# Gated attention and MLP: where the last weights land, and when small steps of the schedule are issued

## The chip, the cores and the metric

The kernel runs on one core of a Trainium2 chip. A core has a matrix engine (TensorE, "PE" in the profile; its weight loads are listed apart as "PEld"), a vector engine (VectorE, "DVE"), a scalar engine for activations (ScalarE, "ACT"), GpSimd ("POOL"), and a queue processor (SyncE, "SP") that in this kernel issues nearly all DMA transfers. Sixteen DMA engines move the data. The engines run their own instruction streams in order and wait for each other by semaphores. The metric is the device time of one execution, in microseconds (us), as the median of several runs.

## What is computed

The input is one sequence of 2048 tokens of width 576. The output mixes softmax attention with 32 heads of 18 and a layer-normed MLP of hidden width 4608, token by token, by a sigmoid gate:

```
x = A_x
g = _sigmoid((x * gate_w).sum(-1, keepdims=True))
a = _A_ref(x, A_wqkv, A_wo)                       # softmax(q k^T / sqrt(18)) v, then @ wo
b = _B_ref(x, B_w1, B_b1, B_w2, B_b2)             # layernorm, gelu(y @ w1 + b1) @ w2 + b2
return g * a + (1 - g) * b
```

## The kernel before

Everything is float32 in and out. Where TensorE multiplies two activations or weights, each of them is split into a rounded part ("hi", type fp32r) and the remainder ("lo"), and three products hi x hi, lo x hi, hi x lo are summed.

**Attention.** The loop at the end of the kernel runs over 32 units u (16 pairs of heads, each in two halves of 1024 queries) and 16 steps kc of 128 keys: 512 steps. Scores are computed twice. Pass 1 (`s1_round`, L197) is only for the row maxima, which DVE reduces from PSUM (L199); `s1_finish` gathers them (L207 to L210), `rows` transposes them (L214), ACT copies the transpose to the tile `mr` (L216), and DMAs write it into rows 54 and 55, and 118 and 119, of the unit's query tile `qa` (the helper `dma_r`, L112). With these rows pass 2 (`s2`, L238) yields scores with the maximum already subtracted, ACT takes the exponential (L240) into one of three buffers ("p" and "ring"), and `pv` (L255) multiplies with the values. When a unit is done, `o_store` copies its result (`oe`, L267), extracts the denominators by DMA (`dn<-oe`, L269), stores the numerators (L275) and some slots later takes the reciprocal on DVE (`spread`, L278), stores it (L279, `dn_scr`), and again some slots later spreads it over the rows of a scratch tensor (`wide`, L287).

**MLP.** It is written as a generator, `mlp()`, whose pieces fill PE between the attention's matmuls. It goes over 4 blocks of 512 tokens and in each over 9 groups of 4 chunks of 128 hidden units. A group has two up pairs q (`h_pair`, L433, 64x512 matmuls against the tile `big` that holds the normalised tokens) and four down tiles (`out_pair`, L513, accumulated by DVE at L522 in `x`). GELU is done by ACT (L484, L486) and POOL (helper `pool_op`, L153), which leaves `hh` and `hl`. In the first block the weights come raw from the input, and `split` prepares them: ACT rounds (L357, tile `w`), POOL subtracts (L153), the result serves the current block and is also stored in a scratch tensor (L362, `w_scr`) from which the other three blocks load it (`reload`, issued through L112, 1152 KB for an up pair, 576 KB for a down chunk). Up weights live in buffers of the pool `wp1`, down weights in those of `wp2`. Raw up weights are loaded at L336 into one half of a tile `x`, raw down weights at L342 into the other.

**What sets the order.** Every engine's order is the order in which the Python program emits instructions; nothing is rearranged. Three devices decide it. `run_due()` is called some four times per step and counts slots; `defer(n, f)` runs f at the n-th slot from now. `bg` is a list of weight splits: `run_due` takes one when the modelled end of POOL's work is near enough (`pool_end - now < queue`) and the slot that was written down when the raw weights were loaded, plus a constant, is reached (`LAND`, 8 slots, for up weights; `LAND - 2` for down weights). `ready()` takes entries at once when PE is about to use their result. `fill()` advances the MLP by one piece; when the MLP is used up it appends the output projection, `out_proj` (L1020 matmuls, its weights loaded at L880 and split at L873 and L874, its result combined with the MLP's by DVE at L1024).

SP's queue holds all the loads and stores in program order. Eight semaphores are used in turn for their completion, so that an issue waits for the transfer eight before it.

Of the kernel before, what the change touches and what calls it, by code (L numbers as in the profile page):

```python
# [8 lines left out]
F32 = mybir.dt.float32  # L9
F32R = mybir.dt.float32r  # L10
AF = mybir.ActivationFunctionType
# [5 lines left out]
P = 128  # L17
S = 2048
D = 576
# [3 lines left out]
NT = S // P  # L23
# [14 lines left out]
LEAD = 4  # L38
FILL = 1100.0
SLOT = 950.0  # L40
LAND = 8
GAP = 1130.0
TOTAL = NB * NG * (G // 2 * 27 * 231 + 8 * 3 * G * 131)
PLAN = [[(), (0,), (1,), (2,), (3,), (4,), (5, 6), ()], [(), (), (0,), (1,), (2,), (3,), (4,), (5, 6)],
# [2 lines left out]
PSTEP = (489, 494, 497, 499)  # L47
# [10 lines left out]
def gated_mix_kernel(ctx: ExitStack, tc: tile.TileContext, x, wqkv, wo, w1, b1, w2, b2, gate_w, out):  # L58
    nc = tc.nc
# [12 lines left out]
    w2_scr = dram.tile([NFC, P, 2, D], F32, name="w2_scr")  # L72
# [25 lines left out]
    def psum(pool):  # L98
        return pool.tile([P, TB], F32, name="ps")
# [10 lines left out]
    def dma_r(queue, dst, src):  # L110

        queue.dma_start(dst.bitcast(F32), src)  # L112


    slot = [0]
    later = []

    def defer(n, fn):
        later.append((slot[0] + n, fn))


    bg = []
# [27 lines left out]
    def pool_op(n, fn, *args, **kw):  # L150

        pool_end[0] = max(pool_end[0], now[0]) + n * (1.36 if fn == nc.gpsimd.tensor_scalar else 2.7)
        fn(*args, **kw)  # L153


    NU = 2 * NPAIR
# [5 lines left out]
    def unit(u):  # L162
        return UNITS[u]
# [37 lines left out]
    def s1_finish(u):  # L201

        m4 = M4.pop(u)
        nm = asm.tile([P, 2, 8], F32, name="nm")
        nm2 = asm.tile([P, 2, 2, 8], F32, name="nm2")
        nmh = asm.tile([P, 2, 8], F32R, name="nmh")
        nc.vector.tensor_reduce(nm, m4, axis=AX.X, op=ALU.max, negate=True)  # L207
        nc.vector.tensor_copy(nmh, nm)
        nc.vector.tensor_copy(nm2[:, :, 0, :], nmh.bitcast(F32))
        nc.vector.tensor_tensor(nm2[:, :, 1, :], nm, nmh.bitcast(F32), op=ALU.subtract)  # L210

        def rows():
            ps = psum(ps_s1)
            nc.tensor.transpose(ps[:32, :P], nm2.rearrange("p a b c -> p (a b c)"), ident)  # L214
            mr = asm.tile([32, P], F32R, name="mr", bufs=1)
            nc.scalar.activation(mr, ps[:32, :P], AF.Copy)  # L216
            qa = QA[u % 3]
            for h in range(2):
                for b in range(2):
                    r = 64 * h + 54 + b  # L220
                    k = (h * 2 + b) * 8
                    dma_r(nc.sync, qa[r:r + 1, :].rearrange("o (t n) -> o t n", n=P), mr[k:k + 8, :].bitcast(F32))
        if looped[0]:
            ROWS.append(rows)
        else:
            defer(2, rows)
# [35 lines left out]
    def o_store(u, ps):  # L262

        pair, half = unit(u)
        oe = asm.tile([P, TB], F32, name="oe", bufs=1)
        dn = asm.tile([P, 16], F32, name="dn", bufs=1)
        nc.vector.tensor_copy(oe, ps)  # L267
        cols = slice(2 * pair * DH, 2 * (pair + 1) * DH)
        nc.sync.dma_start(dn, oe[DH::32, :])  # L269
        for h in range(2):  # L270
            for qb in range(2):
                c = 32 * (2 * h + qb)
                d = (2 * pair + h) * DH
                q = half * HALF + qb * TB
                nc.sync.dma_start(ot_scr[0, d:d + DH, q:q + TB], oe[c:c + DH, :])  # L275

        def spread():
            nc.vector.reciprocal(dn, dn)  # L278
            nc.sync.dma_start(dn_scr[u], dn)  # L279
            if u < NU - 1:  # L280
                defer(16 if u < NU - 2 else 4, wide)
            else:
                hooks[0]()

        def wide():
            dst = ot_scr[1, cols, half * HALF:(half + 1) * HALF]
            nc.sync.dma_start(dst.rearrange("(h d) n -> h d n", d=DH), dn_scr[u][:, None, :].to_broadcast([2, DH, HALF]))  # L287
            stored.append(u)
        if u < NU - 1:
            defer(12 if u < NU - 2 else 4, spread)  # L290
        else:
            spread()

# [4 lines left out]
    looped = [False]  # L298
# [9 lines left out]
    def mlp():  # L308
        W1, W2, HT = {}, {}, {}
        RAW = {}  # L310
        seq = [(tb, g) for tb in range(NB) for g in range(NG)]
        n = len(seq)
# [3 lines left out]
        def chunk(q):  # L316

            i, m = divmod(q, G // 2)
            return i, m, seq[i][1] * G + 2 * m
# [5 lines left out]
        LOADED = {}  # L325
        NQ0 = npair // NB

        def load_w1(q):

            if (1, q) in LOADED or q >= NQ0:  # L330
                return
            LOADED[1, q] = slot[0] + (LAND if looped[0] else 5)
            fc = chunk(q)[2]
            for h in range(2):
                src = w1[:, (fc + h) * P:(fc + h + 1) * P]
                nc.sync.dma_start(R1[64 * h:64 * h + 64], src.rearrange("(c p) n -> p c n", p=64))  # L336

        def load_w2(c):
            if (2, c) in LOADED or c >= NFC:
                return  # L340
            LOADED[2, c] = slot[0] + (LAND - 2 if looped[0] else 3)
            nc.sync.dma_start(R2[c % 2], w2[c * P:(c + 1) * P, :])  # L342

        def rounded(dst, src):
# [7 lines left out]
        def split(table, key, pool, shape, raw, src, scr, then):  # L352

            def first():
                LOAD[raw[0]](raw[1])
                t = pool.tile(shape, F32R, name="w" + str(len(shape)))
                nc.scalar.activation(t[:, 0], src, AF.Copy)  # L357
                bg.insert(0, (any_time, lambda: second(t), queue))

            def second(t):  # L360
                pool_op(src.free_size(), nc.gpsimd.tensor_tensor, t[:, 1], src, t[:, 0].bitcast(F32), op=ALU.subtract)
                defer(4 if looped[0] else 20, lambda: nc.sync.dma_start(scr, t.bitcast(F32)))  # L362
                defer(3 if looped[0] else 1 if raw != (1, 2) else 16, lambda: then(raw[1]))
                table[key] = (t[:, 0], t[:, 1])

            queue = raw[0] ** 2 * SLOT
            bg.append((lambda: LOADED.get(raw, slot[0] + 1), first, queue))

        def reload(table, key, pool, shape, scr):
            t = pool.tile(shape, F32R, name=f"w{len(shape)}")  # L370
            dma_r(nc.sync, t, scr)
            table[key] = (t[:, 0], t[:, 1])
# [8 lines left out]
        def prep(upto):  # L381

            while asked[0] <= min(upto, npair - 1):
                q = asked[0]
                asked[0] += 1
                shape = [P, 2, 9, P]
                if q >= NQ0:
                    reload(W1, q, wp1, shape, w1_scr[q % NQ0])
                    continue
                split(W1, q, wp1, shape, (1, q), R1, w1_scr[q], lambda q: load_w1(q + 1))  # L390

        def prep_w2(i):
            for m in range(G // 2):
# [172 lines left out]
        def pair(q, ahead, last=False, inner=False):  # L566
            prep(q + ahead)
            yield from h_pair(q, last, inner)
            i, m, _ = chunk(q)
            if m == 1 and seq[i][1] == NG - 1:  # L570
                hidden[0] = seq[i][0]

        for i in range(n + 1):
            q = 2 * i
            inside = i < n and seq[i][1] == NG - 1
            held = 1 if 0 < i < n and seq[i][1] == 0 else 2
            if i < n:
                yield from pair(q, held, last=i > 0)  # L580
                prep(q + 1 + held)
            if i > 0:
                yield from outs(i - 1, pair(q + 1, 2, inner=True) if inside else ())
            if 0 < i < n:
                prep_w2(i)
            if i < n and not inside:
                yield from pair(q + 1, held)

    stream = [mlp()]
    spent = [0.0]  # L590
# [4 lines left out]
    kept = [0]  # L595

    def atom():

        while stream:
            try:  # L600
                spent[0] += next(stream[0])
            except StopIteration:
                stream.pop(0)
                return 0
            if cut[0]:
                end, cut[0] = cut[0], 0
                return end
        return 0
# [15 lines left out]
    with ExitStack() as a:  # L624
# [172 lines left out]
        for tb in range(NB):  # L797
            work = [(qk_group, (tb, mt)) for mt in (range(9) if tb < 2 else (4, 0, 1, 2, 3, 5, 6, 7, 8))] + [(v_group, (tb, t, n)) for t in range(4) for n in range(2)]
            for g, (fn, args) in enumerate(work):
                if tb == 0:  # L800
                    if g in W_AT:
                        n = W_AT[g]
# [19 lines left out]
                if tb == NB - 1:  # L822
# [5 lines left out]
                    if g == 9:  # L828
                        qkstack.close()
                        wp1 = mstack.enter_context(tc.tile_pool(name="m_w1", bufs=3))  # L830
# [211 lines left out]
    proj = out_proj()  # L1042
    over = [None]

    def fill(step, share):

        if over[0] is None:
            piece[0] = share
            behind[0] = base + (TOTAL - base) * step / FIN
            t = spent[0]  # L1050
            atom()
            run_due(max(spent[0] - t, GAP))
            if not stream and kept[0] == NT and step > PSTEP[-1] + 1:
                stream.append(proj)
                over[0] = step
                spent[0] = 0.0
        else:
            filler(spent[0] + FILL)
            run_due()

    looped[0] = True
    for u in range(NU):
        for kc in range(NT):
            step = u * NT + kc
# [63 lines left out]
```

## Time and profile before

| | us |
|---|---|
| time, median of 3 runs | 2394.49 |
| the runs | 2390.41, 2395.73, 2394.49 |
| span of the profiled execution | 2390.7 |
| the profiled execution's own time | not listed apart from the three runs |
| PE busy in the span | 2319.4 |
| DVE, ACT, POOL busy | 1650.7, 1364.9, 966.2 |
| mean granted PE clock | 0.99 |

The span runs from the first to the last instruction that the profiler recorded. A row of the timeline has the start, the duration, the engine, the line, the operation, what it writes and reads, the number of instructions that it stands for, and in brackets the idle time of that engine before it and what ended it. A row of the windows has the stretch, its length, the busy time of PE, PEld, DVE, ACT and POOL with counts, then the mean granted clock of PE (1.00 is full), the busy share of the DMA engines and the rate of the transfers in GB/s. "SPq" rows are issues of transfers; their duration is the time that the issue held SP's queue.

### The profile page before, as it was taken

The page shows a single profiled execution, that of the slowest core. Times are in us where ns is not written, and L with a number is a line of the kernel's source. Part 1 is how long each engine was busy: PE and PEld are TensorE (multiplying, and loading weights), DVE is VectorE, ACT ScalarE, POOL GpSimd, SP SyncE. Part 2 cuts the span into 40 slices and gives each one's busy share as a digit, 9 for nine tenths or more (in the row PEclk, how much of TensorE's full clock was granted, in tenths as well). Part 3 has the DMA queues.
Part 4 walks back from the last instruction along what each step waited for, and adds up shares of the span by engine and source line. Part 5 has one row for each costly group of instructions (what it writes and reads, how often), then busy time and mean ns, then how long its engine had stood idle before and what let it go on. Part 6 is the DMA issues. An engine that isn't in the chain of part 4 may idle for free.

```text
span 2390.7 us, 50629 instructions
## 1 busy us (share of the span) xinstructions
PE 2319.4 (97%) x20585; PEld 1620.3 (68%) x20585; DVE 1650.7 (69%) x2890; ACT 1364.9 (57%) x1604; POOL 966.2 (40%) x964
## 2 busy tenths in 40 slices
PE   8999899999999999999999999999999999999899
PEld 7876566666666666666666666666666666666558
DVE  5466577777776777777777777777767777777534
ACT  4222366666665666666566666666555665666552
POOL 3001366666654433333353444443344333444500
PEclk9999899999999999999999999999999999999999
DMA  7748744435456423243263424232454342332254
GB/s 231 242 165 230 210 153 131 164 130 148 133 185 162 155 93 116 93 131 115 76 167 140 145 91 135 93 115 93 121 156 145 110 121 108 105 110 79 90 185 156
DMA packets 164866, 330.25 MB, mean 138 GB/s; under 512 B 57898, under 2 KB 84558, under 8 KB 153906
## 3 DMA queue, kind: packets, MB, share of 16 engines
q1 hardware_dynamic: 163050, 323.78, 43.3%
q8 instruction: 162, 2.65, 0.5%
q10 hardware_dynamic: 1584, 3.24, 0.4%
q14 instruction: 70, 0.57, 0.1%
HBM read 234.16 MB, written 96.58 MB: 138 GB/s over the span
## 4 chain that ended last, share of the span: by engine, by line
PE 90%; DVE 4%; DMA 3%; ACT 2%; issue 1%; SPq 0%; ACTq 0%; DVEq 0%; POOL 0%
PE ps L513 20%; PE ps L255 19%; PE ps L433 18%; PE pss L238 12%; PE ps L197 11%; PE ps L745 4%; PE ps L1020 2%; PE ps L766 2%; DVE m L199 1%; DMA big<-y_scr 1%; PE ps L672 1%; DMA dn<-oe 1%; ACT w L357 0%; DMA qa<-mr 0%; DVE p L732 0%
## 5 line engine op out<-in xcount | busy, mean ns | idle before, releaser
L199 DVE TENSOR_REDUCE m<-ps 128x1 f32<-128x512 f32 x2048 | 1297.4, 684 | 459.2 <-PE ps L197 457.3
L240 ACT ACTIVATE p<-pss 128x1024 f32<-128x1024 f32 x684 | 701.5, 1026 | 493.4 <-PE pss L238 484.0
L153 POOL TENSOR_SCALAR zz<-zz 128x512 f32<-128x512 f32 x288 | 178.8, 621 | 858.0 <-ACT zz L486 849.0
L433 PE MATMUL ps<-big,w 64*128 64x512 f32 x3888 | 518.1, 393 | 0.1
L513 PE MATMUL ps<-w,hh 64*128 64x288 f32 x4352 | 499.0, 299 | 19.1 <-DMA w<-w_scr 7.1
L238 PE MATMUL pss<-qa,ka 56*128 56x512 f32 x2048 | 481.8, 437 | 20.3 <-ACT p L240 12.4
L240 ACT ACTIVATE ring<-pss 128x1024 f32<-128x1024 f32 x340 | 348.7, 1026 | 243.5 <-PE pss L238 238.6
L197 PE MATMUL ps<-ka,qa 54*128 54x512 f32 x2048 | 461.5, 410 | 15.4 <-DVE m L199 9.2
L513 PEld LDWEIGHTS ps<-w,hh 64*128 64x128 f32 x4352 | 400.0, 186 | 76.7 <-issue 51.9
L433 PEld LDWEIGHTS ps<-big,w 64*128 64x128 f32 x3888 | 392.5, 186 | 66.8 <-DVE z L453 0.4
L238 PEld LDWEIGHTS pss<-qa,ka 56*128 56x128 f32 x2048 | 198.3, 185 | 271.1 <-ACT p L240 126.1
L153 POOL TENSOR_TENSOR zz<-zz,z 128x512 f32<-128x512 f32 x288 | 371.6, 1290 | 24.0
L513 PE MATMUL ps<-w,hl 64*128 64x288 f32 x2176 | 350.7, 292 | 0.0
L255 PE MATMUL ps<-p,vt 128*32 128x512 f32 x2736 | 347.3, 603 | 0.0
L197 PEld LDWEIGHTS ps<-ka,qa 54*128 54x128 f32 x2048 | 240.3, 186 | 49.7 <-DVE m L199 22.6
L513 PEld LDWEIGHTS ps<-w,hl 64*128 64x128 f32 x2176 | 235.5, 185 | 0.2
L153 POOL TENSOR_TENSOR w<-x,w 128x576 fp32r<-128x576 f32 (+1 forms) x54 | 98.5, 1839 | 322.9 <-ACT w L357 321.3
L153 POOL TENSOR_TENSOR hl<-zz,hh 128x512 fp32r<-128x512 f32 x136 | 176.9, 1301 | 11.4
L255 PE MATMUL ps<-ring,vt 128*32 128x512 f32 x1360 | 179.1, 598 | 0.0
L255 PEld LDWEIGHTS ps<-p,vt 128*32 128x32 f32 x2736 | 71.7, 109 | 150.3 <-issue 149.9
L522 DVE SCALAR_TENSOR_TENSOR x<-ps,x 128x288 f32<-128x288 f32 x256 | 105.1, 452 | 40.6 <-PE ps L513 27.6
L745 PE MATMUL ps<-big,wqk 128*128 128x512 f32 x432 | 111.9, 408 | 2.1 <-ACT wqk L666 1.6
(98 smaller groups left out, 1374.7 us busy)
## 6 DMA issues: line engine op xcount, KB each, us to landing
w<-w_scr SPq DMA_DIRECT2D x54, 1152.0 KB
w<-w_scr SPq DMA_DIRECT2D x108, 576.0 KB
x<-in_B_w_dram SPq DMA_DIRECT2D x72, 288.0 KB
w_scr<-w SPq DMA_DIRECT2D x18, 1152.0 KB
w_scr<-w SPq DMA_DIRECT2D x36, 576.0 KB
big<-y_scr SPq DMA_DIRECT2D x42, 384.0 KB
qa<-qk_scr SPq DMA_DIRECT2D x192, 72.0 KB
ka<-qk_scr SPq DMA_DIRECT2D x84, 144.0 KB
```

The lines of the kernel that those rows point to most:

```text
L153: fn(*args, **kw)
L197: nc.tensor.matmul(ps, qa[r0:r0 + 54, t * P:(t + 1) * P], ka[r0:r0 + 54, kb * TB:(kb + 1) * TB], start=True, stop=True)
L199: nc.vector.tensor_reduce(M4[u][:, h, t, kb:kb + 1], ps, axis=AX.X, op=ALU.max)
L238: nc.tensor.matmul(ps[:, h, :], ka[r0:r0 + 56, kc * P:(kc + 1) * P], qa[r0:r0 + 56, qb * TB:(qb + 1) * TB], start=True, stop=True)
L240: nc.scalar.activation(RING[n % 3][:, qb], ps, AF.Exp, scale=SCALE)
L255: nc.tensor.matmul(OB[u][r:r + 32, :], v[:, k, 19 * h:19 * h + 32], RING[c % 3][:, qb, h, :], start=(k == 0), stop=(k == NT - 1))
L433: nc.tensor.matmul(ps[h], wt[w_][r, c, :], Y[s_][r, c, :], start=(k == 0), stop=(k == 26))
L513: nc.tensor.matmul(ps[nn][:, :ND], h_[r, tok], w_[p_][r, cs[nn]], start=(k == 0), stop=(k == 6 * G - 1))
L522: nc.vector.scalar_tensor_tensor(dst, ps[nn][:, :ND], 0.5, b2b[:, cs[nn]] if g == 0 else dst, op0=ALU.mult, op1=ALU.add)
L745: nc.tensor.matmul(ps, w_[:, c, ms], big[:, s_, :], start=(k == 0), stop=False)
L766: nc.tensor.matmul(ps[:, :ND], big[:, s_, tok], w_[:, c, cs], start=(k == 0), stop=False)
L1020: nc.tensor.matmul(ps[:, :ND], OT[b][2][:, s_, tok], w_part(w_, c)[:, cs], start=(k == 0), stop=(k == 13))
```

## The change

1. The down weights of the very last group (four chunks of 576 KB) are no longer loaded by `prep_w2` into buffers of `wp2` but by a new function, `borrow_w2`, into two buffers of `wp1`, as soon as the up weights that were there have been used.
2. `LAND` goes from 8 to 11 slots for raw up weights and stays at 6 for raw down weights. ACT's rounding of an up pair is done in two pieces, 5 of 9 columns of blocks and, two slots later, the other 4; POOL's subtraction is queued behind the second piece.
3. The reciprocal of the denominators is taken 20 slots after the unit's end, not 12 (but for the last units).
4. The maxima of a unit go to `qa` in two transfers of 16 rows of 512 bytes, not four of 8.
5. `fill()` checks before its work, not behind it, whether the MLP is used up, so that the output projection starts one call earlier.

```diff
--- before.py
+++ after.py
@@ -38,7 +38,7 @@
 LEAD = 4
 FILL = 1100.0
 SLOT = 950.0
-LAND = 8
+LAND = 11
 GAP = 1130.0
 TOTAL = NB * NG * (G // 2 * 27 * 231 + 8 * 3 * G * 131)
 PLAN = [[(), (0,), (1,), (2,), (3,), (4,), (5, 6), ()], [(), (), (0,), (1,), (2,), (3,), (4,), (5, 6)],
@@ -216,10 +216,8 @@
             nc.scalar.activation(mr, ps[:32, :P], AF.Copy)
             qa = QA[u % 3]
             for h in range(2):
-                for b in range(2):
-                    r = 64 * h + 54 + b
-                    k = (h * 2 + b) * 8
-                    dma_r(nc.sync, qa[r:r + 1, :].rearrange("o (t n) -> o t n", n=P), mr[k:k + 8, :].bitcast(F32))
+                r = 64 * h + 54
+                dma_r(nc.sync, qa[r:r + 2, :].rearrange("b (t n) -> b t n", n=P), mr[16 * h:16 * h + 16, :].bitcast(F32))
         if looped[0]:
             ROWS.append(rows)
         else:
@@ -287,7 +285,7 @@
             nc.sync.dma_start(dst.rearrange("(h d) n -> h d n", d=DH), dn_scr[u][:, None, :].to_broadcast([2, DH, HALF]))
             stored.append(u)
         if u < NU - 1:
-            defer(12 if u < NU - 2 else 4, spread)
+            defer(20 if u < NU - 2 else 4, spread)
         else:
             spread()
 
@@ -338,7 +336,7 @@
         def load_w2(c):
             if (2, c) in LOADED or c >= NFC:
                 return
-            LOADED[2, c] = slot[0] + (LAND - 2 if looped[0] else 3)
+            LOADED[2, c] = slot[0] + (LAND - 5 if looped[0] else 3)
             nc.sync.dma_start(R2[c % 2], w2[c * P:(c + 1) * P, :])
 
         def rounded(dst, src):
@@ -354,7 +352,15 @@
             def first():
                 LOAD[raw[0]](raw[1])
                 t = pool.tile(shape, F32R, name="w" + str(len(shape)))
+                if looped[0] and raw[0] == 1:
+                    nc.scalar.activation(t[:, 0, :5], src[:, :5], AF.Copy)
+                    defer(2, lambda: rest(t))
+                    return
                 nc.scalar.activation(t[:, 0], src, AF.Copy)
+                bg.insert(0, (any_time, lambda: second(t), queue))
+
+            def rest(t):
+                nc.scalar.activation(t[:, 0, 5:], src[:, 5:], AF.Copy)
                 bg.insert(0, (any_time, lambda: second(t), queue))
 
             def second(t):
@@ -388,6 +394,14 @@
                     reload(W1, q, wp1, shape, w1_scr[q % NQ0])
                     continue
                 split(W1, q, wp1, shape, (1, q), R1, w1_scr[q], lambda q: load_w1(q + 1))
+
+        def borrow_w2(q):
+
+            t = wp1.tile([P, 2, 9, P], F32R, name="w4").rearrange("p a b c -> p (a b c)")
+            for j in range(2):
+                part = t[:, 2 * j * D:2 * (j + 1) * D].rearrange("p (a d) -> p a d", d=D)
+                dma_r(nc.sync, part, w2_scr[2 * (q % NQ0) + j])
+                W2[q, j] = (part[:, 0], part[:, 1])
 
         def prep_w2(i):
             for m in range(G // 2):
@@ -569,6 +583,8 @@
             i, m, _ = chunk(q)
             if m == 1 and seq[i][1] == NG - 1:
                 hidden[0] = seq[i][0]
+                if i == n - 1:
+                    defer(1, lambda: borrow_w2(q))
 
 
 
@@ -579,9 +595,11 @@
             if i < n:
                 yield from pair(q, held, last=i > 0)
                 prep(q + 1 + held)
+                if i == n - 1:
+                    borrow_w2(q)
             if i > 0:
                 yield from outs(i - 1, pair(q + 1, 2, inner=True) if inside else ())
-            if 0 < i < n:
+            if 0 < i < n - 1:
                 prep_w2(i)
             if i < n and not inside:
                 yield from pair(q + 1, held)
@@ -1044,16 +1062,16 @@
 
     def fill(step, share):
 
+        if over[0] is None and not stream and kept[0] == NT and step > PSTEP[-1] + 1:
+            stream.append(proj)
+            over[0] = step
+            spent[0] = 0.0
         if over[0] is None:
             piece[0] = share
             behind[0] = base + (TOTAL - base) * step / FIN
             t = spent[0]
             atom()
             run_due(max(spent[0] - t, GAP))
-            if not stream and kept[0] == NT and step > PSTEP[-1] + 1:
-                stream.append(proj)
-                over[0] = step
-                spent[0] = 0.0
         else:
             filler(spent[0] + FILL)
             run_due()
```

## The prediction

> **What bounds the kernel now.** I read the page first, for the engine that sets the time.
>
> ```profile
> span 2390.7 us, 50629 instructions
> PE 2319.4 (97%) x20585; PEld 1620.3 (68%) x20585; DVE 1650.7 (69%) x2890; ACT 1364.9 (57%) x1604; POOL 966.2 (40%) x964
> PE 90%; DVE 4%; DMA 3%; ACT 2%; issue 1%; SPq 0%; ACTq 0%; DVEq 0%; POOL 0%
> ```
>
> TensorE (PE) is busy for 97% of the span and is 90% of the chain that ended last. The change takes no matmul away, so it can only gain where PE stands still. The table of windows of 50 us shows where that is.
>
> ```profile
> 250.00:300.00 50.00, 41.91 (x277) 26.67 (x277) 25.84 (x42) 21.85 (x26) 20.47 (x20) 0.84 0.83 230
> 700.00:750.00 50.00, 45.07 (x427) 29.63 (x425) 32.92 (x58) 27.13 (x33) 24.44 (x26) 0.95 0.57 132
> 1700.00:1750.00 50.00, 49.67 (x477) 34.43 (x475) 36.21 (x64) 32.15 (x38) 32.11 (x34) 1.00 0.68 161
> 1750.00:1800.00 50.00, 45.80 (x430) 30.35 (x428) 34.39 (x59) 27.13 (x29) 13.84 (x16) 0.97 0.36 114
> 2250.00:2300.00 50.00, 37.52 (x350) 24.22 (x346) 14.98 (x30) 22.81 (x27) 16.48 (x17) 0.86 0.37 125
> ```
>
> The second number of a row is the window, the third PE's busy time, the third from the end the granted clock. A normal window has 49.67 of 50. Four windows have less, and each has a lower clock. The timeline names what PE waited for in each.
>
> ```profile
> 295.06 1.16 ACT L357 ACTIVATE w<-x 128x1152 fp32r<-128x1152 f32 x1 [6.13 <-DMA x<-in_B_w_dram]
> 297.19 0.79 PE L238 MATMUL pss<-qa,ka 56*128 56x512 f32 x2 [5.68 <-ACT p L240]
> 745.28 0.25 DVE L278 RECIPROCAL dn<-dn 128x16 f32<-128x16 f32 x1 [5.93 <-DMA dn<-oe]
> 746.13 0.79 PE L197 MATMUL ps<-ka,qa 54*128 54x512 f32 x1 [4.50 <-DVE m L199]
> 1755.21 1.17 PE L238 MATMUL pss<-qa,ka 56*128 56x512 f32 x2 [3.87 <-DMA qa<-mr]
> 2263.15 0.85 PE L513 MATMUL ps<-w,hh 64*128 64x288 f32 x4 [6.81 <-DMA w<-w_scr]
> 2269.00 0.61 PE L513 MATMUL ps<-w,w 64*128 64x288 f32 x2 [3.41 <-DMA w<-w_scr]
> ```
>
> In brackets stand the idle time before the instruction and what ended it. I name the stalls D (raw up weights, 5.68 us), B (reciprocal, 4.50), C (maxima rows, 3.87) and A (last down weights, 6.81 and 3.41). Each is followed by slow matmuls:
>
> ```profile
> 746.00:750.00 4.00, 3.87 (x19) 1.09 (x19) 2.60 (x6) 1.02 (x1) 0.00 (x0) 0.50 0.26 82
> 750.00:752.00 2.00, 2.00 (x14) 0.98 (x8) 0.02 (x1) 0.25 (x1) 0.00 (x0) 0.58 0.00 0
> 1756.00:1758.00 2.00, 2.00 (x9) 0.40 (x12) 0.00 (x0) 1.02 (x1) 0.00 (x0) 0.50 0.00 0
> 2261.00:2273.00 12.00, 6.10 (x38) 4.96 (x40) 0.00 (x0) 1.09 (x2) 2.11 (x3) 0.50 0.79 293
> ```
>
> Behind B, 4 us at 0.50 and 2 us at 0.58 lose 2.0 + 0.84 = 2.8 us, so B costs 4.5 + 2.8 = 7.3. Behind C at least 1.0 is lost: 4.9. A stall of about 4 us thus costs 5 to 7 here.
>
> **The change, part by part.** PE's order is written out by the program and hardly changes. So I give every moved instruction the time at which PE, in the profile before, passed the point where the program now emits it.
>
> *Reciprocal 12 to 20 slots later (B).* The row at 745.28 blocks DVE's queue for 5.93 us; the maxima reductions (L199) that PE needs stand behind it. Its data are late because its transfer was issued behind twelve loads of the next block:
>
> ```profile
> 720.93 10.32 SPq L112 DMA_DIRECT2D big<-y_scr  x12
> 732.50 0.60 SPq L269 DMA_DIRECT2D dn<-oe  x1
> ```
>
> Eight slots are two steps, 7.4 us, more than the 5.93. But a store of split weights (L362, 1152 KB) now falls between the loads, about 3 us more before dn lands. Of the 7.4 some 4.4 are left, and DVE still waits about 1.5; PE stood 1.4 less than DVE (5.93 against 4.50), so nearly all is covered. B gives -7.0 (-5 to -7.3). The shift of dn_scr and of the wide load behind it meets no reader for tens of us.
>
> *Maxima rows in two transfers (C).* 64 issues fewer, and SP is not the bound. At C the rows were late because of their place in the queue:
>
> ```profile
> 1730.40 10.54 SPq L112 DMA_DIRECT2D big<-y_scr  x12
> 1742.17 6.60 SPq L112 DMA_DIRECT2D qa<-mr  x4
> DMA packets 64, 0.02 MB, mean 6 GB/s; under 512 B 32, under 2 KB 64, under 8 KB 64
> ```
>
> They are issued behind the same twelve loads as before, and land when those are through. The change leaves that order alone, so C stays: -0.4 (0 to -0.8, at most one issue's 6.60/4 = 1.65 less some overlap). The third row is the DMA view of 1228.5 to 1231.3 us, where four such transfers run alone: 64 packets, 32 of data and 32 under 512 B, which are completions, so eight engines wrote one each per transfer. The Trainium skill's "DMA: Bandwidth & Descriptors" (section "Why a DMA increments its semaphore by 16 and not by 1") says that a transfer is spread over the largest number up to 16 that divides the outermost sizes of both sides; the old 8 agrees, and the new shape, outermost 2, would have two engines with eight rows each. That speaks against the merge; by it C would give 0 in place of -0.4.
>
> *Raw up weights read three slots later, in halves (D, F, G).* At D the load is issued at the same place, and the first rounding is emitted at the same place too: there the modelled backlog of GpSimd (POOL), not the landing count, holds it. So the stall at 297.19 stays; the first piece is shorter, 128x640 for 128x1152, 1.16 x 640/1152 = 0.64: D gives -0.3 (0 to -0.5). The change does not do there what it says.
>
> Two places get worse by it. F: the load for the 17th split stood ahead of a unit's q, k and v loads, and now comes behind them.
>
> ```profile
> 411.51 0.39 SPq L183 DMA_DIRECT2D vt<-v_scr  x1
> 412.00 6.57 SPq L342 DMA_DIRECT2D x<-in_B_w_dram  x2
> 664.47 1.36 SPq L336 DMA_DIRECT2D x<-in_B_w_dram  x2
> 671.60 0.39 SPq L183 DMA_DIRECT2D vt<-v_scr  x1
> ```
>
> The rows near 412 show a raw load right behind v: its issue took 6.57 us. After the change the issue begins 1.36 before 671.99, at 670.6, ends at 677.2 by that row, and its 590 KB need another 2 us at the 293 GB/s of the window above: about 679.2. ScalarE (ACT) is to round it where PE passes 674.7, so ACT waits about 4.5, and the exponentials behind it, and PE, about 4 (at D 5.68 for 6.13). With the slow clock that is +6 (0 to +8; 0 if v drains sooner).
>
> G: the last split waits for POOL's backlog at 718.9, the position at which PE starts on that very pair.
>
> ```profile
> 670.41 1.16 ACT L357 ACTIVATE w<-x 128x1152 fp32r<-128x1152 f32 x1
> 671.65 2.67 POOL L153 TENSOR_TENSOR w<-x,w 128x1152 fp32r<-128x1152 f32 x1 [7.23 <-ACT w L357]
> 718.88 2.26 PE L433 MATMUL ps<-big,w 64*128 64x512 f32 x18
> 718.90 1.03 ACT L240 ACTIVATE ring<-pss 128x1024 f32<-128x1024 f32 x1 [1.27 <-PE pss L238]
> ```
>
> Before it was done 45 us ahead (674.3). Now ACT's second piece comes behind the exponential that ends at 719.93 and takes 1.16 x 512/1152 = 0.5, then POOL needs 2.67: 723.2. PE needs the result from its third matmul, at 719.2: idle 4, with the clock +6 (+5 to +7). Elsewhere the raw loads keep 10 us and more to their reading, and the halves hide nothing, since no PE wait stands there.
>
> *Last down weights into up weights' places (A).* The four loads leave the place at 2259 and go out when PE is done with the last up pairs. The weights are then in place, and POOL is late next:
>
> ```profile
> 2221.87 0.41 SPq L880 DMA_DIRECT2D x<-in_A_wo_dram  x1
> 2235.94 2.26 PE L433 MATMUL ps<-big,w 64*128 64x512 f32 x18
> 2244.55 0.67 POOL L873 TENSOR_SCALAR big<-x 128x576 fp32r<-128x576 f32 x1
> 2262.02 1.26 POOL L153 TENSOR_TENSOR w<-zz,w 128x512 fp32r<-128x512 f32 x1
> 2269.80 1.43 PE L513 MATMUL ps<-w,w 64*128 64x288 f32 x10
> ```
>
> The second pair of loads must wait for the buffer that PE releases at 2238.2, and the output projection's load (2221.87) now stands behind it in SP's queue. 1.18 MB and then 1.18 MB at 293 GB/s are 8.1 us, and the issues about 1: POOL's L873 starts at 2247.5 and not at 2244.55, and all behind it moves by 3.0. The last hidden part is ready at 2263.3 + 3.0 = 2266.3, and PE's first output tile ends about 2267.0 in place of 2271.23: -4.3 (-2 to -7.5, the latter without the delay of POOL).
>
> *Projection started one fill earlier (E).* It fills waits on exponentials, the longest of 1.46 us. But only three accumulators, 42 matmuls, can be filled before the row of DVE:
>
> ```profile
> 2300.91 0.50 PE L238 MATMUL pss<-qa,ka 56*128 56x512 f32 x2 [1.46 <-ACT ring L240]
> 2311.02 1.22 PE L1020 MATMUL ps<-big 128*128 128x288 f32 x8
> 2315.57 0.94 DVE L1024 SCALAR_TENSOR_TENSOR res<-ps,gate,bt 128x288 f32<-128x288 f32 x2 [14.41 <-DMA bt<-b_scr]
> ```
>
> At the end of the second row 36 matmuls were done. With nine more ahead PE comes to its 43rd at about 2312.1, ahead of weighted sums of values (estimated 2.3 us) that until now it did before 2315.57, and stands 3.5 us. It is then behind by those sums: +2.3 (from -1.4, nine matmuls of 1.22/8 = 0.15 gone from the end, to +4 with the slow clock). The trace has full clock after 1.46 and 0.50 after 3.87, nothing between. The Trainium skill's "TensorE: Matmul & The Clock Gate" (section "Part 1: The HAM clock gate") gives one idle window of about 3.4 us that runs free; by it 3.5 us would rarely fill a window, and E stays at +2.3.
>
> *Sum:* A -4.3, B -7.0, C -0.4, D -0.3, E +2.3, F +6, G +6: +2.3, taken as +2. The page's span is 2390.7; its execution's own time isn't given, and the three times have a median of 2394.49, 3.8 above the span. Both would move by 2: **2396.5 us**. One part in 500 (0.2%, 4.8 us) is about what a measurement of this kernel can tell from no change.
>
> **The rivals.** *All four stalls go.* For it: each part is aimed at one. A 13.5 (10.2 idle and 3.1 of slow clock from 6.10 busy at 0.50), B 7.3, C 4.9, D about 6, without F and G: -20 to -32, about 2368. Against it: the places of D's and C's issues don't move. Chance 0.12.
>
> *F does not come and A pays in full.* v drains sooner with no raw load before it, and POOL isn't late: 2.3 - 6 - 3.2 = -6.9, 2387.5 (2383 to 2389.5). Against it the 6.57 row. Chance 0.21.
>
> *POOL becomes the bound at the end of the MLP, slower.* If the borrowed weights and the projection's load move at the 161 GB/s of the normal window and not at 293, they take 14.7 us and not 8.1, POOL starts 6.6 later still, and the first output tile ends at 2273.5, 2 later than before: A +2, sum +8.6, 2403. It decides from a landing 4.2 later than I take, at 2251.7, where A's gain is gone. For it: 293 stood in a window with nothing else in flight. Chance 0.27.
>
> **How the numbers follow.** My forecast has the other 0.40: 0.27 of it within 4.8 us, 0.09 above, 0.04 below. Faster: 0.04 + 0.12 + 0.21 = 0.37. Slower: 0.09 + 0.27 = 0.36. Same: 0.27. The lower bounds of all terms give -12 and the upper ones +13, not all at once; the range 2384 to 2407 takes in the second and third rival and leaves out the first and the outer ends. Within the likeliest case alone it is 2391 to 2402.
>
> **What would show it.** Right: the wait before L278 near 745 under 2 us and no PE idle; waits of some 4 us before PE near 297, 1755 and, new, near 676 (behind a rounding that waits for x) and 720 (behind POOL's subtraction); near 2260 PE waiting for POOL and not for w<-w_scr; L1024's first wait unchanged and PE's behind it above 2 us. Wrong: no new idle near 676 or 720, which takes 6 off each; C or D gone; or L513 waiting past 2271.

## The result, and the profile after

| | before | after |
|---|---|---|
| median, us (8 runs each) | 2393.86 | 2403.07 |
| lowest to highest, us | 2388.37 to 2399.05 | 2398.33 to 2405.42 |
| span of the profiled execution, us | 2390.7 | 2403.6 (time 2405.42) |

The ratio is 1.0039 (95% interval 1.0028 to 1.0051): the change makes the kernel slower by 9.2 us. The profiled spans lie 12.9 us apart. Every sign by which the prediction was to be known as right is in the trace after the change; two further losses (H) and the size of two terms are what it missed.

To see where, I put the matmuls of the second score pass of both traces side by side, 2048 in the same order in each, and took how much later each starts after the change. The table has the steps of that delay (worked out from the two traces; us).

| place (us after the change) | predicted | step of the delay |
|---|---|---|
| start to 272 | none | +2.9 |
| D, to 313 | -0.3 | +0.6 |
| H, to 368 and to 645 (not predicted) | 0 | +3.5 and +2.2 |
| F, to 709 | +6 | +7.0 |
| G, to 749 | +6 | +6.6 |
| B, to 772 | -7.0 | -7.5 |
| C, to 1780 | -0.4 | -0.2 |
| A, to 2290 | -4.3 | -6.4 |
| E, to 2335 | +2.3 | +5.1 |
| behind it | 0 | -1.0 |

Seen in the windows of 50 us after the change:

```profile
300.00:350.00 50.00, 47.25 (x445) 32.77 (x449) 35.35 (x58) 29.74 (x37) 23.30 (x20) 0.96 0.19 57
350.00:400.00 50.00, 47.77 (x455) 31.35 (x447) 35.62 (x65) 33.03 (x40) 28.27 (x27) 0.97 0.40 139
650.00:700.00 50.00, 45.31 (x430) 31.08 (x430) 33.15 (x59) 28.37 (x35) 22.75 (x19) 0.97 0.39 93
700.00:750.00 50.00, 43.98 (x373) 29.21 (x374) 30.02 (x52) 28.95 (x37) 28.23 (x27) 0.93 0.50 173
1750.00:1800.00 50.00, 46.29 (x417) 29.73 (x415) 33.52 (x56) 28.93 (x34) 19.53 (x21) 0.93 0.66 170
2250.00:2300.00 50.00, 44.62 (x423) 28.91 (x419) 18.96 (x35) 25.49 (x28) 23.91 (x25) 0.93 0.21 66
2300.00:2350.00 50.00, 43.98 (x306) 27.16 (x302) 17.53 (x30) 29.45 (x35) 1.64 (x1) 0.97 0.59 192
```

Before the change PE was busy for 49.33 and 49.03 us in the two windows from 300 to 400, for 49.11 from 650 to 700 and for 47.55 from 2300 to 2350; 2250 to 2300 was 37.52 and is 44.62. The timeline after the change shows what PE waits for. First the stalls that the change was to remove, D, B, C and A:

```profile
298.57 0.74 ACT L356 ACTIVATE w<-x 128x640 fp32r<-128x640 f32 x1 [6.73 <-DMA x<-in_B_w_dram]
300.28 0.80 PE L236 MATMUL pss<-qa,ka 56*128 56x512 f32 x2 [5.85 <-ACT p L238]
769.63 0.24 DVE L276 RECIPROCAL dn<-dn 128x16 f32<-128x16 f32 x1
1769.01 1.18 PE L236 MATMUL pss<-qa,ka 56*128 56x512 f32 x2 [3.36 <-DMA qa<-mr]
2242.29 0.43 SPq L898 DMA_DIRECT2D x<-in_A_wo_dram  x1
2259.44 0.67 POOL L891 TENSOR_SCALAR big<-x 128x576 fp32r<-128x576 f32 x1
2276.93 0.57 PE L527 MATMUL ps<-w,w 64*128 64x288 f32 x4 [2.24 <-POOL w L153]
```

D is as long as before (5.68), C nearly (3.87). The reciprocal waits no more. At A, PE waits for POOL and not for weights; POOL's L891 is 14.89 later than before (2244.55), no more than PE's matmuls there (14.9), so POOL is not held up by the projection's weights. Then the new ones, F, G, H and E:

```profile
677.88 0.39 SPq L183 DMA_DIRECT2D vt<-v_scr  x1
678.37 8.69 SPq L334 DMA_DIRECT2D x<-in_B_w_dram  x2
691.07 0.74 ACT L356 ACTIVATE w<-x 128x640 fp32r<-128x640 f32 x1 [6.29 <-DMA x<-in_B_w_dram]
692.77 0.50 PE L236 MATMUL pss<-qa,ka 56*128 56x512 f32 x2 [4.26 <-ACT p L238]
736.01 0.62 ACT L363 ACTIVATE w<-x 128x512 fp32r<-128x512 f32 x1
736.71 2.61 POOL L153 TENSOR_TENSOR w<-x,w 128x1152 fp32r<-128x1152 f32 x1 [6.03 <-ACT w L363]
739.37 2.93 PE L447 MATMUL ps<-big,w 64*128 64x512 f32 x12 [3.91 <-POOL w L153]
708.88 0.50 PE L236 MATMUL pss<-qa,ka 56*128 56x512 f32 x2 [1.85 <-ACT p L238]
355.65 1.40 ACT L359 ACTIVATE w<-x 128x576 fp32r<-128x576 f32 x2 [0.99 <-DMA x<-in_B_w_dram]
358.54 0.49 PE L236 MATMUL pss<-qa,ka 56*128 56x512 f32 x2 [1.90 <-ACT p L238]
2324.04 0.94 DVE L1042 SCALAR_TENSOR_TENSOR res<-ps,gate,bt 128x288 f32<-128x288 f32 x2 [14.52 <-DMA bt<-b_scr]
2324.61 0.72 PE L1038 MATMUL ps<-big 128*128 128x288 f32 x3 [4.25 <-DVE res L1042]
```

F: the raw up load, right behind v, held SP for 8.69 us, and ACT and then PE waited. G: PE waits for POOL's subtraction, which waits for ACT's second piece. The last two rows are E. H: ACT waits for raw down weights. SP's rows and the row of the reading show why, first before the change, then (last three rows) after it:

```profile
340.30 2.06 SPq L112 DMA_DIRECT2D qa<-qk_scr  x6
342.46 1.68 SPq L342 DMA_DIRECT2D x<-in_B_w_dram  x2
350.53 1.25 ACT L357 ACTIVATE w<-x 128x576 fp32r<-128x576 f32 x2
346.52 1.69 SPq L334 DMA_DIRECT2D x<-in_B_w_dram  x2
348.25 0.64 SPq L368 DMA_DIRECT2D w_scr<-w  x1
348.99 1.73 SPq L340 DMA_DIRECT2D x<-in_B_w_dram  x2
```

Before, the raw down load goes out right behind the loads of q (340.30) and is read 8.07 us after its issue, without a wait. After the change the raw up load (L334) and the store of a split (L368, 1152 KB) stand between them. They hold SP's queue for 2.47 us (346.52 to 348.99), and the down load (L340) goes out that much nearer to its reading: ACT is ready for it at 354.66, 5.67 us after its issue, and gets it at 355.65, 6.66 us after. So the place in the queue is enough to explain this wait; whether the transfer itself is slower too, the traces don't show.

Two entries of the table hold something else too. Of the +3.5 to 368, 0.5 comes at 324, where PE's transposition of the maxima (L214) waits 1.44 us for DVE; the three other kernels with the second piece have that wait too (1.41 to 1.42), and none without it. And of the +7.0 to 709, 1.2 comes behind the wait at 708.88, which is of the kind of H: ACT waits there (0.94 us, at 705.99) for raw down weights whose load went out behind an up load and a store. F by itself is +5.8.

### The profile page after: what moved, and what is told of

Its sections match the earlier page's. It is cut to its first block, busy times and chain, and to the rows that moved or that the text cites. A ratio compares the mean times of both kernels' runs of the same rounds, so it can differ in the third digit from the quotient of the medians.

```text
span 2403.6 us, 50504 instructions
## 1 busy us (share of the span) xinstructions
PE 2326.2 (97%) x20585; PEld 1623.4 (68%) x20585; DVE 1653.0 (69%) x2890; ACT 1369.4 (57%) x1619; POOL 967.1 (40%) x964
## 4 chain that ended last, share of the span: by engine, by line
PE 72%; issue 9%; POOL 6%; DMA 6%; DVE 3%; ACT 2%; SPq 1%; POOLq 0%; ACTq 0%; DVEq 0%
PE ps L527 16%; PE ps L253 15%; PE ps L447 13%; PE pss L236 10%; PE ps L197 9%; DMA x<-in_B_w_dram 4%; PE ps L763 4%; POOL zz L153 3%; PE ps L784 2%; PE ps L1038 2%; POOL w L153 2%; DVE m L199 1%; POOL hl L153 1%; SPq L334 1%; ACT p L238 1%
## 5 line engine op out<-in xcount | busy, mean ns | idle before, releaser
L527 PE MATMUL ps<-w,hh 64*128 64x288 f32 x4352 | 497.9, 299 | 11.7
```

The lines of the kernel that those rows point to most:

```text
L527: nc.tensor.matmul(ps[nn][:, :ND], h_[r, tok], w_[p_][r, cs[nn]], start=(k == 0), stop=(k == 6 * G - 1))
```

## The experiments

All times are medians; each run was compared with the kernel before on the same chip (its medians were 2394.6, 2394.2 and 2394.9 in the three sets).

| kernel | us | ratio, 95% interval |
|---|---|---|
| part 1 alone, borrowed weights | 2390.48 | 0.9981 (0.9969 to 0.9993) |
| part 2 alone, count 11 and two pieces | 2416.48 | 1.0091 (1.0074 to 1.0108) |
| part 3 alone, reciprocal | 2389.85 | 0.9980 (0.9968 to 0.9992) |
| part 4 alone, rows in two transfers | 2390.53 | 0.9986 (0.9975 to 0.9997) |
| part 5 alone, projection earlier | 2397.21 | 1.0011 (1.0001 to 1.0021) |
| count 11, one piece | 2392.84 | 0.9993 (0.9984 to 1.0002) |
| count 8, two pieces | 2420.80 | 1.0114 (1.0100 to 1.0128) |
| part 2, v loaded later | 2410.37 | 1.0073 (1.0059 to 1.0086) |
| the change, one piece | 2382.32 | 0.9952 (0.9940 to 0.9964) |
| parts 1, 3, 4 | 2379.71 | 0.9943 (0.9930 to 0.9955) |
| the same, denominators earlier | 2380.38 | 0.9943 (0.9931 to 0.9955) |
| the same, part 5, bt earlier | 2378.44 | 0.9935 (0.9923 to 0.9947) |

**Each part by itself.** The edits are those of the change, one at a time.

*Part 2 alone.* 

> The kernel before with part 2 alone (landing count 11 for raw up weights, 6 for raw down weights as before, ACT's rounding in two pieces). Theory from the two traces, laid side by side matmul by matmul: part 2 costs +7 near 680 us (F), +6.5 near 720 (G), and a third loss that the prediction did not have, H, some +6.5 in all at the seven places between 350 and 650 us where raw down weights are rounded: about +20 us, ratio 1.008, with the stall at 745 (B) still there. Rival 1, the prediction's sizes: F and G alone, +12, ratio 1.005. Rival 2: G needs the later reciprocal or the merged rows as well (SP's queue in another order): then no wait for POOL before the up pair near 720 and +14 or less.

It measured +21.9, as the theory had it. B stands, and is longer, since the shifted store lies ahead of dn's load; the first row is G:

```profile
737.94 3.48 PE L441 MATMUL ps<-big,w 64*128 64x512 f32 x16 [3.91 <-POOL w L153]
767.88 0.25 DVE L278 RECIPROCAL dn<-dn 128x16 f32<-128x16 f32 x1 [8.26 <-DMA dn<-oe]
768.74 0.79 PE L197 MATMUL ps<-ka,qa 54*128 54x512 f32 x1 [6.81 <-DVE m L199]
```

G is 3.91 here as in the complete change, so it needs none of the other parts.

*Part 1 alone.* 

> The kernel before with part 1 alone (last down weights in up weights' places). Theory: POOL's last splits bound this place behind the weights, -6 us (ratio 0.9975), waits of some 4.5 us in all for POOL's subtraction before the last hidden products near 2263, first output tile 4 to 5 us earlier. Rival, the prediction's third: POOL is held by the projection's weights and starts on them 3 us or more later than 2244.55: -4 to +2 us.

-4.1. PE waits for POOL (first row) and not for weights, and the matmuls behind that place are 6.5 us earlier against those in front of it. POOL is not late. But in the profiled execution all of it is lost again by 2313, behind DVE's and ACT's work on the denominators:

```profile
2263.02 0.85 PE L521 MATMUL ps<-w,w 64*128 64x288 f32 x4 [2.24 <-POOL w L153]
2290.59 1.90 DVE L959 TENSOR_TENSOR x<-x,ka 128x512 f32<-128x512 f32 x3 [6.13 <-DMA ka<-ot_scr]
2293.51 0.79 PE L238 MATMUL pss<-qa,ka 56*128 56x512 f32 x2 [2.58 <-ACT p L240]
```

The profiled execution took 2392.85 us, 2.4 over the median of this kernel, and another took 2378.89. Whether all executions lose as much at this place is not shown.

*Part 3 alone.* 

> The kernel before with part 3 alone (reciprocal 20 slots after the unit's end). Theory: the stall at 746 goes with its slow clock, -7.3 us, ratio 0.997. Rival: in the old order of the queue, without part 2, dn<-oe is issued at 732.5 and the reductions stall there anyway for another transfer: 0 to -3 us.

-4.8, and no PE wait of 0.9 us or more near 746: the stall went with 7.5 us between the same matmuls. Here too the place near 2293 (PE 2.17) takes most of it back in the profiled execution, which is the slowest of the twelve (2392.86).

*Part 5 alone.* 

> The kernel before with part 5 alone (projection one call earlier). Theory: PE comes to the 43rd matmul of the projection before bt has landed and stands about 4 us there, +5 us (ratio 1.002), with DVE's L1024 still starting when bt lands. Rival: the price at that place comes from the borrowed weights' order in the complete change (bt issued later), and alone the earlier start gives -1 us by filling two waits for exponentials.

+2.6, smaller than expected but of that sign (the interval just leaves out no change). The place itself is as in the complete change, so the borrowed weights have no part in it:

```profile
2312.87 0.94 DVE L1024 SCALAR_TENSOR_TENSOR res<-ps,gate,bt 128x288 f32<-128x288 f32 x2 [14.49 <-DMA bt<-b_scr]
2313.44 1.09 PE L1020 MATMUL ps<-big 128*128 128x288 f32 x3 [4.23 <-DVE res L1024]
```

*Part 4 alone.* 

> The kernel before with part 4 alone (maxima rows in two transfers of 16 rows). Theory: 0 (ratio 0.999 to 1.001); the stall near 1755 stays within 1 us of 3.9, since the rows stand behind the same twelve loads. Rival 1: half as many issues bring the rows 1 to 2 us earlier there and the slow clock behind that stall goes: -3 to -5. Rival 2: a transfer now uses two DMA engines and not eight and is late elsewhere: +2 or more.

-3.6, more than the theory's 0, and not for the reason of rival 1: C is still 3.13 us. The rows show another place, A:

```profile
2255.26 1.42 SPq L112 DMA_DIRECT2D qa<-mr  x2
2256.77 1.76 SPq L112 DMA_DIRECT2D w<-w_scr  x4
2260.77 0.85 PE L511 MATMUL ps<-w,hh 64*128 64x288 f32 x4 [5.42 <-DMA w<-w_scr]
2265.09 0.61 PE L511 MATMUL ps<-w,w 64*128 64x288 f32 x2 [1.89 <-DMA w<-w_scr]
```

Two issues instead of four stand ahead of the weights (1.42 us in place of 2.79), and PE's waits of 6.81 and 3.41 are 5.42 and 1.89. That the first is 1.4 shorter goes with the 1.37 us saved in the queue: it is 6.76 to 6.89 in the seven kernels that load these weights at this place behind four issues. The second is no sign of part 4: with part 5 alone, which has the four issues (2.78 us), it is 1.90. So about 1.4 us of the gain is located, and the rest of the 3.6 (interval 0.7 to 6.0) is not.

**What in part 2 costs.** Two kernels take its two edits apart, and one takes away what F's load stands behind. The cuts show what tells each kernel apart; a line of dots stands for lines left out, and the words behind # are not in the kernel.

```diff
-LAND = 8                                  # count 11, one piece: the rounding as before
+LAND = 11
...
```

> The kernel before with the landing count 11 for raw up weights, but ACT's rounding in one piece. Theory: the losses of part 2 come from the two further slots that the second piece takes, not from the three slots of the count. The program's order then has the 17th raw up load ahead of v again (at 662.8 us of the profile before), the last split at 672.9 and no raw up load right ahead of a raw down load: F, G and H all go, 0 against the kernel before (ratio 0.999 to 1.001). Rival: the later reading is the cause, and the pieces are harmless: +12 to +21.

-1.3, no difference that can be measured. F, G and H are gone, though the weights are read later (the rounding of 670.41 is at 675.62).

```diff
+                if looped[0] and raw[0] == 1:      # count 8, two pieces
+                    nc.scalar.activation(t[:, 0, :5], src[:, :5], AF.Copy)
+                    defer(2, lambda: rest(t))
+                    return
...
```

> The kernel before with ACT's rounding in two pieces, but the old landing count 8. Theory: F stays and is dearer by the 2.3 us that the rounding is earlier (672.4 for 674.7, raw load behind v as with part 2): +8 to +9; G stays: +6; H goes, since no raw up load stands right ahead of a raw down load between 350 and 650 us: about +15 (ratio 1.006). Rival: the landing count is the cause: 0 to +2.

+26.6. The sign is the theory's, the size is missed: F is an idle of 8.62 us, because ACT reads earlier and the load is no earlier. From 360 to 650 us the delay doesn't grow, so the steady part of H is gone as expected, but the loss ahead of 358 is there (some 4 us), which I had not placed. ACT waits there for raw down weights too (1.25 and 0.60 us): the up load (342.88) and the store (344.23) stand here too ahead of the down load, which goes out at 349.60, behind the loads of q.

```profile
686.08 0.74 ACT L358 ACTIVATE w<-x 128x640 fp32r<-128x640 f32 x1 [9.11 <-DMA x<-in_B_w_dram]
687.78 0.79 PE L238 MATMUL pss<-qa,ka 56*128 56x512 f32 x2 [8.62 <-ACT p L240]
```

```diff
-                    load_v(u // 2 + 1)             # at kc == 1
+            if kc == 4 and u % 2 == 0 and u // 2 + 1 < NPAIR:
+                load_v(u // 2 + 1)                 # against part 2 alone
```

> Part 2 alone again, but the loads of v are issued three steps later (at kc 4 and not kc 1), so that no raw up load stands behind v. Theory: F goes, no PE idle of 3 us or more near 690 us; G and H stay; some 7 us less than part 2 alone (2416.5), near 2410. Rival: F is the landing of raw weights by itself, whatever stands ahead: no change against part 2 alone.

6.1 us less than part 2 alone (5.7 if each is taken against the kernel before in its own set, with intervals that overlap), near the 7 expected, but not by F alone: from 272 to 368 us the delay falls by 0.9 us where it grew by 2.9. SP is no longer held (1.35 for 7.27 us in part 2 alone), PE's idle at F is 1.79 and not 3.55, and the delay grows by 4.6 there and not by 6.6. ACT still waits:

```profile
672.58 1.35 SPq L336 DMA_DIRECT2D x<-in_B_w_dram  x2
683.12 0.74 ACT L358 ACTIVATE w<-x 128x640 fp32r<-128x640 f32 x1 [3.82 <-DMA x<-in_B_w_dram]
684.82 0.49 PE L238 MATMUL pss<-qa,ka 56*128 56x512 f32 x2 [1.79 <-ACT p L240]
```

So v in front is part of F. The load stands behind q and k too and comes 10.5 us after its issue; what fills these 10.5 us is not shown.

**The change without what costs.** 

> The complete change, but ACT's rounding in one piece. Theory: the second piece alone turns the change from a gain into a loss: F, G and H go, and the 20 us that part 2 costs by itself come back, about 2384 (ratio 0.996), with the waits of some 4 us near 692 and 739 gone. Rival: without them another wait takes their place (the stall at the reciprocal returns, or the order of SP's queue with three slots more is late elsewhere), and it stays at 2395 or more.

-12.5. With the rounding in one piece the change gains, and the second piece costs 20.7 us in it (2403.07 against 2382.32, in different sets; 21.7 if each is taken against the kernel before in its own set). No PE wait of 0.9 us stands between 300 and 1740.

*Parts 1, 3 and 4* (no part 2, no part 5). 

> Parts 1, 3 and 4 alone (borrowed weights, later reciprocal, rows in two transfers). Theory 1, the gains add: -4.1 - 4.8 - 3.6 = -12.5, 2382 (ratio 0.995). Theory 2, the end gives a part back: PE, earlier by some 12 us, stands for the denominators (DVE's L947 on ka<-ot_scr, then ACT's L240) near 2290, with the slow clock some 5 us, as in the runs of part 1 and part 3 alone: -8 to -10, 2385.

-15.1. Nearly nothing is taken back near 2290 (0.6 us): DVE's wait there is 3.25 us and PE has only two of 1.18. Theory 2 fails for this kernel. The sum of the single gains is met within the interval (10.8 to 16.8), but not as three gains that add: in the trace B gives 7.5 and A 6.5, C nothing, and the weights at A for which part 4 alone shortened a wait are no longer loaded there. What part 4 adds to the other two is not shown.

```diff
-PSTEP = (489, 494, 497, 499)
+PSTEP = (489, 494, 496, 499)
```

> Parts 1, 3 and 4, and the denominators of the projection's first block loaded one step earlier (496 in place of 497). If theory 2 of the run before holds, DVE's wait for ka<-ot_scr shortens by some 3.7 us, PE's wait of 2 us or more near 2290 goes and so does the slow clock: 3 to 5 us below parts 1, 3 and 4. If the denominators are not it: no change.

2380.38 against 2379.71: no change. DVE's wait is gone and nothing follows, since PE had no wait for it to lose. Why DVE had the same transfer 8.0 and 7.7 us after its issue in the runs of parts 1 and 3 alone, and 5.5 us after it with parts 1, 3 and 4, stays open.

```diff
+        load_b(0)
         load_o(1)
         load_den(1)
-        load_b(0)
```

> As the run before, with part 5 too (projection one call earlier) and with bt loaded ahead of the second block's numerators and denominators instead of behind them. If part 5 loses because PE's 43rd projection matmul waits for bt, then bt lands some 5 us earlier, that wait of 4 us goes, and the two waits for exponentials of 1.2 us are filled: 1 to 3 us below the run before. Rival: the second block's loads, now later, stop PE further on: no gain, or a loss of up to 4.

2378.44, 1.9 us lower, with intervals that overlap: not told apart from the run before. The mechanism shows, though. DVE's wait for bt is 5.15 in place of 14.46 us, PE no longer waits for DVE (4.28 in the change with one piece), and a new wait of 1.90 stands further on:

```profile
2291.22 0.52 DVE L1034 SCALAR_TENSOR_TENSOR res<-ps,gate,bt 128x288 f32<-128x288 f32 x1 [5.15 <-DMA bt<-b_scr]
2301.68 0.50 PE L236 MATMUL pss<-qa,ka 56*128 56x512 f32 x2 [1.90 <-ACT p L238]
```

This is what the rival said: ACT, ahead of that exponential, waits 2.87 us for the second block's denominators, which are now loaded behind bt.

## Why the prediction was right or wrong

The range (2384 to 2407) holds 2403.07, but the likeliest case was within 0.2% and the time is 0.39% above. The account of mechanisms was right for most places. One term was missing (H) and two were too small (A, a gain, and E, a loss). That the range held is in part luck: H and E together add 8.5 us, and A's larger gain takes 2.1 of them off.

- **D** was right: the count does not move the rounding there, and the stall is 5.85 us.
- **B** was right: -7.5 for -7.0, and no wait at the reciprocal is left.
- **C** was right: 3.36 for 3.87. The sentence that fewer issues are worth little because SP is not the bound was wrong at A, where part 4 alone shortened PE's first wait by 1.4 us.
- **F** and **G** were right in place, in what waits, and nearly in size: +7.0 for +6 (5.8 without the wait at 708.88), +6.6 for +6. Parts of F were larger than I had them: the issue held SP for 8.69 us and not 6.57, and ACT waited 6.29 and not 4.5. I laid them on later reading and pieces together; the runs show that the pieces alone make them.
- **H** is the step that failed: "Elsewhere the raw loads keep 10 us and more to their reading, and the halves hide nothing, since no PE wait stands there". I followed the raw up loads to their own readers and not to the raw down loads behind them in the same queue. Nor was it so before the change: the down load of 342.46 was read 8.07 us after its issue, and 2.47 us more of issues ahead of it were enough for a wait. The stretches of H were worth +5.7, where I had 0; that they come from the second piece is shown (they are gone with the count alone), and the place in the queue is read from the rows.
- **A** was undersized, -6.4 for -4.3, because the assumed 3 us of delay on POOL did not come. The second pair of borrowed loads went out right ahead of the projection's weights, at 2241.39; less the delay of 14.9 at that place this is 2226.5 in the times before, 11.7 us ahead of the release at 2238.2 for which I made it wait.
- **E** was right in mechanism, +5.1 for +2.3: the idle was 4.25 us and not 3.5, and slow clock came with it (0.91 in the window 2320 to 2340 of the trace after; in the trace before it was 1.00), so the upper bound of +4 was the nearer one. The Trainium skill's "TensorE: Matmul & The Clock Gate" (section "Part 1: The HAM clock gate") with its one idle window of about 3.4 us, by which E was to stay at +2.3, does not settle it: here a window need not be idle throughout (last section).
- The rule of the Trainium skill's "DMA: Bandwidth & Descriptors" (section "Why a DMA increments its semaphore by 16 and not by 1") on spreading a transfer was right about the mechanism, and what I made of it, that it speaks against the merge, was not. This is the DMA view of 1243.5 to 1244.9 us after the change, with two transfers:

```profile
DMA packets 36, 0.02 MB, mean 12 GB/s; under 512 B 4, under 2 KB 36, under 8 KB 36
```

32 data packets and 4 completions are two engines for each, where eight were before; the time of part 4 alone is none the worse for it.
- The third rival, POOL as the bound at the end of the MLP, had the right sign and the wrong cause: POOL was on time, and that its 2403 meets the measured time is chance. The first rival's gain is not what the change brought, but -15.1 was there in its parts 1, 3 and 4.

## What to carry to other kernels

A step that is split in two takes a later slot for its second half, and everything chained behind it (the subtraction, the store, the next load) moves by that much in every queue it uses; follow each of these to the next reader, also of other data. Where one queue carries all transfers, ask of each shifted load what now stands ahead of it and what now stands behind it. Parts of a bundled change with opposite signs should be run alone: here three gain 15 us together and part 2 alone loses 22.

## What the runs showed that I had not expected

Executions differ before the steady loop. The run of part 3 has the same program as before up to the first reciprocal that it moves, near 350 us, and yet the same matmul is 2.0 us later at this point:

```profile
258.15 0.80 PE L238 MATMUL pss<-qa,ka 56*128 56x512 f32 x2 [1.25 <-ACT p L240]
260.15 0.80 PE L238 MATMUL pss<-qa,ka 56*128 56x512 f32 x2 [1.25 <-ACT p L240]
```

The first row is of the kernel before, the second of part 3 alone. Between 215 and 265 us PE waits often and shortly, and the granted clock differs from run to run (in the window 245 to 255 it was 0.84 before and 0.66 with part 3). The +2.9 at the start of the table is of this size (in the other twelve kernels the delay at 272 us is 0.0 to 3.0), and I do not lay it on the change; it is part of why the two profiled spans lie further apart (12.9) than the medians (9.2).

A PE stall need not be 3.4 us long to be followed by the slow clock, and its length alone does not decide. The wait of 1.79 us with v loaded later (684.82) was followed by it, a longer one in the kernel with count 8 and two pieces was not. The first two windows are of the one, the last two of the other, with its stall between them:

```profile
682.42:685.83 3.41, 1.62 (x14) 1.04 (x12) 1.29 (x2) 2.71 (x5) 0.46 (x1) 1.00 0.84 239
685.83:689.25 3.42, 3.42 (x18) 2.70 (x16) 0.17 (x1) 1.52 (x3) 3.42 (x2) 0.50 0.07 13
357.89 0.50 PE L238 MATMUL pss<-qa,ka 56*128 56x512 f32 x2 [2.72 <-ACT p L240]
353.60:357.01 3.41, 1.57 (x14) 1.05 (x10) 2.44 (x4) 1.97 (x4) 2.21 (x3) 1.00 1.00 374
357.01:360.43 3.42, 2.54 (x20) 0.86 (x22) 0.00 (x0) 2.37 (x3) 3.25 (x4) 1.00 0.78 218
```

The windows are those at whose edges the granted clock changes: in all 14 traces, every complete stretch of one clock is a whole multiple of 3.413 us long (a slow one 3.41, 6.83, 10.24 or 13.65). I went through these windows from the 265th us on, where the clock was full, and took PE's busy share in each. All 71 with a share of 0.45 or less were followed by a window at half clock, 6 of 21 between 0.45 and 0.55, and none of the 8480 above. So in these traces a stall slows the clock when it leaves PE busy for less than about half of one such window. The 2.72 us fell on two windows (1.57 and 2.54 us busy of 3.41), the 1.79 us wholly into one (1.62). Two waits of 1.18 us can do it as well: with parts 1, 3 and 4 they left 1.05 us in the window 2286.23 to 2289.64, and the next was at 0.50. The length of the window agrees with the Trainium skill's "TensorE: Matmul & The Clock Gate" (section "Part 1: The HAM clock gate"), which has one idle window of about 3.4 us that runs free; that it must be idle throughout does not agree, and here the measurement decides. A step on ACT that costs PE 2 us can therefore cost 3.5: at the 1.79 us the delay grew from 3.5 to 7.0.
